# Tail scores of two heads from one shared low-part product, with the decay added by VectorE and head 1's operands stacked by GpSimd

## The chip, the cores and the metric

The kernel runs on one core of a Trainium2 chip. The metric is the device time of one execution in microseconds (us), the median of several runs. The engines are TensorE (PE in the profile), VectorE (DVE), ScalarE (ACT), GpSimd (POOL) and SyncE (SP, which here issues nearly all transfers).

## What is computed

Attention with a forget gate over 8 batches, 8 heads, 576 tokens and head size 64, and a mixing block with a feed-forward part on its output:

```
scores = (q @ k.T) / 8
cum    = cumsum(log(clip(f, 1e-4, 1)))                 # per head and token
scores = where(causal, -1e9, scores + cum[row] - cum[column])
attn   = softmax(scores); x = attn @ v                 # heads side by side: x is (8, 576, 512)
h      = (x.T @ U @ V).T;  u = x + h
out    = u + relu(u @ w_ch1) @ w_ch2
```

Results have the precision of float32. Where the kernel multiplies in the faster type fp32r, it splits an operand into a high part and the rest (the low part), and adds up the products.

## The kernel before, in words

Two heads of a batch make a pair; there are 32 pairs, p = 0 to 31. One call of `step(t)` is made of ten slots (`s`) and works on three pairs at once: scores of pair t, transposition and first values of the pair before, the rest of the one before that. In every slot PE also gets one unit of the feed-forward part of an earlier batch, where there is one (`filler`), or of a batch's mixing (`mixing`). The order of PE and SP is the order of the code; that of DVE, ACT and POOL comes from a scheduler at build time (SP's as well in steps 1 to 6).

The scores of a head are taken in four blocks of 128 query rows against the keys up to the diagonal (`score`, L379 on). The last 64 tokens of both heads, the **tail**, share one block of 128 rows, head 0 above head 1, against all 576 keys, in two halves of 288 columns (`score_tail`, L405 on; tile `St`).

Pairs 0 to 5 (p < NF = 6) multiply in full precision, from padded tiles `qk` that hold 64 rows of data, one row of ones and one of decay (L364). A tail half takes two products, one a head, which show as two records each. Pairs 6 to 31 multiply in fp32r, from two tiles `G[j]`, one a head, with four planes: plane 0 is the query's high part, plane 2 the key's high part in one half of the partitions and its low part in the other, plane 1 the query's low part and plane 3 the key's high part, with four rows of ones and decay in the free half (`parts`, L332 on, `place_decay`, L348 on). L367 multiplies planes 0 and 2, L368 planes 1 and 3. A tail half takes four such products, two a head. `parts` fills the planes by casts (L330, on ACT, or all on POOL in six steps) and subtractions on POOL (L345, L346). The decay rows come from the internal tensor `cumd` by SP (L351).

DVE then adds the mask, takes the row minimum of the negated scores and writes the sum back (L388, tail L414), ACT exponentiates (L396, tail L424) and frees the bank. In the first seven steps DVE also decodes the feed-forward weights (L72 to L89) from 64-bit words.

Of the kernel before, what the change touches and what calls it, by code (L numbers as in the profile page):

```python
# [21 lines left out]
P = 128  # L22
# [15 lines left out]
NX = 3  # L38
NF = 6


@with_exitstack
def tile_decay_attention_moe(ctx, tc, qk, v, f, U, V, w1, w2, out):
# [83 lines left out]
    COLS = tuple(slice(o, o + S) for o in AOFF)  # L127
    mask = att.tile([P, ZR + HW], F32, name="mask")
    nc.vector.memset(mask, 0.0)
    blank = mask[:, 0:256].bitcast(mybir.dt.bfloat16)  # L130
# [11 lines left out]
    def clear_operands():  # L142

        for j in range(2):
            g = G[j].bitcast(F32)
            tc.keep_in_program_order(nc.gpsimd.memset(g[OTH[j], 1, COLS[j]], 0.0))
            tc.keep_in_program_order(nc.gpsimd.memset(g[OTH[j], 3, COLS[j]], 0.0))
            tc.keep_in_program_order(nc.gpsimd.memset(g[ORW[j] : ORW[j] + 4, 1, COLS[j]], 1.0))
            tc.keep_in_program_order(nc.gpsimd.memset(g[ORW[j] : ORW[j] + 4, 3, COLS[j]], 1.0))
            z0 = (AOFF[j] + S) % 640  # L150
            tc.keep_in_program_order(nc.gpsimd.memset(g[:, 0:2, z0 : z0 + 64], 0.0))


    def decay_log():
        fr = sb.tile([B * H, S], F32, tag="xT", name="fr")
        fl = sb.tile([B * H, S], F32, tag="cr", name="fl")
        return fr, fl, G[0][0 : B * H, :, 0:S], sb.tile([B * H, 2, S], F32, tag="VS", name="dq")
# [54 lines left out]
    def load_w(u):  # L212
# [4 lines left out]
        if kind == "w2":  # L217

            spare = xn[NX - 1].rearrange("p c d -> p (c d)").bitcast(I32)
            if fc % 2:  # L220
                raw, a = spare[:, 1536:2560], sb.tile([P, 512], I32, tag="w2a", name=f"stg{u}")
# [94 lines left out]
    def load_v(p):  # L316
        vr = sb.tile([P, NM + 1, P], F32, tag="vr", name=f"vr{p}")
        st[p]["vr"] = vr.rearrange("p c (j d) -> p c j d", j=2)
        nc.sync.dma_start(vr[:, 0:NM], v[p, 0:MAIN].rearrange("(c p) d -> p c d", p=P))
        for r in range(2):  # L320
            nc.sync.dma_start(vr[64 * r : 64 * r + 64, NM], v[p, MAIN:S])

# [9 lines left out]
    def parts(p, j, engines):  # L332
# [12 lines left out]
        pin(el.tensor_tensor(g[oth, 2, cols], k[oth], gf[oth, 2, cols], op=ALU.subtract))  # L345
        pin(em.tensor_tensor(g[own, 1, cols], q[own], gf[own, 0, cols], op=ALU.subtract))  # L346

    def place_decay(p, j, cm=None):  # L348
        o, r = ORW[j], j * B * NHP + p
        if cm is None:  # L350
            nc.sync.dma_start(G[j].bitcast(F32)[o : o + 4, 1:4:2, COLS[j]], cumd[r])  # L351
            return
# [52 lines left out]
    def score_tail(p, x):  # L405
        z = st[p]
        ps = bank_s(p, f"St{p}_{x}")
        cols = slice(hw * x, hw * x + hw)
        for j in range(2):
            qk_mm(ps[:, :hw], p, ATAIL[j], cols, j == 0, j == 1, j)  # L410
        z["tl"].append(ps)

        def top():
            nc.vector.tensor_tensor_reduce(  # L414
                ps[:, :hw], ps[:, :hw], mask[:, x * ZR : x * ZR + hw], scale=-SCALE,
                scalar=3.0e38 if x == 0 else z["nm"][:, 8:9],
# [149 lines left out]
    def values(p, j):  # L566
# [247 lines left out]
    with tc.manual_schedule(engines=None):  # L814
# [43 lines left out]
    def step(t):  # L858
# [11 lines left out]
        for s in range(6 + 2 if last else SLOTS):  # L870
# [839 lines left out]
```

## Time and profile before

| what | value |
|---|---|
| median of 3 runs | 1192.13 us (1192.12 to 1192.14) |
| the profiled execution's own time | 1192.27 us |
| its span in the profile | 1190.5 us |
| instructions in it | 23774 |
| share of the chain that ended last | PE 85%, DVE 8%, ACT 4%, issue 2%, POOL 1% |

The span runs from the first to the last instruction that the profile shows; the own time has some 1.8 us around it. The chain is followed back from the last instruction, at each step to what released it.

### The profile page before, as it was taken

How to read it: one execution, taken by the hardware profiler on the slowest of the kernel's cores; microseconds unless marked ns; L12 is line 12 of the kernel's file. 1: busy time of each engine (PE TensorE's matmuls, PEld its weight loads, DVE VectorE, ACT ScalarE, POOL GpSimd, SP SyncE). 2: the span in 40 equal slices, each digit the busy share in tenths (PEclk: the TensorE clock that was granted, in tenths of full speed). 3: DMA queues.
4: the chain of work that ended last, by engine and by line, in shares of the span. 5: the costliest groups of instructions: out<-in, count | busy, mean ns of one | idle time of the engine just before them, and what ended most of it. 6: DMA issues, size and time to landing. Idle time of an engine off the chain costs nothing.

```text
span 1190.5 us, 23774 instructions
## 1 busy us (share of the span) xinstructions
PE 1173.5 (99%) x8400; PEld 1080.8 (91%) x8400; DVE 906.1 (76%) x2188; ACT 752.7 (63%) x2046; POOL 561.1 (47%) x588
## 2 busy tenths in 40 slices
PE   8999999999999999999999999999999999999998
PEld 5888899999899989989989997788999999999998
DVE  8988777677777677777676699966777767777675
ACT  8887786766868758767765577344454544545443
POOL 3315565546637447555553000024565555555554
PEclk9999999999999999999999999999999999999999
DMA  5754234434426425426332344542424344243421
GB/s 161 196 147 153 78 98 146 116 82 142 121 74 174 114 58 163 111 74 179 82 84 96 108 142 155 155 112 95 131 89 124 97 135 138 94 107 102 130 54 36
DMA packets 81431, 138.47 MB, mean 116 GB/s; under 512 B 8768, under 2 KB 46144, under 8 KB 79264
## 3 DMA queue, kind: packets, MB, share of 16 engines
q1 hardware_dynamic: 79680, 128.16, 36.1%
q0 software_dynamic: 1152, 8.39, 3.8%
q8 instruction: 66, 1.08, 0.4%
q14 instruction: 53, 0.43, 0.1%
q10 hardware_dynamic: 480, 0.40, 0.1%
HBM read 101.08 MB, written 35.78 MB: 115 GB/s over the span
## 4 chain that ended last, share of the span: by engine, by line
PE 85%; DVE 8%; ACT 4%; issue 2%; POOL 1%; DMA 0%; SPq 0%; ACTq 0%; DVEq 0%; POOLq 0%
PE N L1321 12%; PE B L775 12%; PE A L756 11%; PE A L1301 9%; PE B L1301 7%; PE V L579 6%; PE T L467 4%; PE S L367 3%; PE S L368 3%; PE O L1402 2%; PE B L1321 2%; PE V L544 2%; PE Tt L645 2%; PE S L364 1%; PE T_v L485 1%
## 5 line engine op out<-in xcount | busy, mean ns | idle before, releaser
L396 ACT ACTIVATE P<-S,nm 128x128 f32<-128x128 f32 (+3 forms) x256 | 138.0, 541 | 53.7 <-DVE nm L388 52.7
L199 POOL TENSOR_TENSOR hb<-xn,hb 128x256 fp32r<-128x256 f32 x136 | 111.6, 840 | 126.3 <-ACT hb L196 113.4
L388 DVE CUSTOM_DVE_ANT_0 S<-S,mask 128x128 f32<-128x128 f32 (+3 forms) x256 | 125.7, 497 | 52.5 <-PE S L368 48.6
L330 POOL CAST G<-qk 64x576 fp32r<-64x576 f32 (+1 forms) x76 | 50.6, 679 | 172.4 <-PE St L368 63.8
L756 PE MATMUL A<-uh,w1h 128*128 128x256 f32 (+1 forms) x384 | 119.8, 312 | 0.0
L756 PE MATMUL A<-ul,w1h 128*128 128x256 f32 (+1 forms) x384 | 113.6, 296 | 0.0
L756 PE MATMUL A<-uh,w1l 128*128 128x256 f32 (+1 forms) x384 | 113.5, 296 | 0.0
L196 ACT CAST hb<-xn 128x256 fp32r<-128x256 f32 x136 | 51.7, 404 | 84.7 <-DVE xn L1307 45.5
L775 PE MATMUL B<-w2h,hh 128*128 128x512 f32 x216 | 88.2, 408 | 0.0
L446 DVE TENSOR_TENSOR PTl<-T,PTh 128x512 fp32r<-128x512 f32 (+1 forms) x156 | 78.4, 527 | 9.6 <-ACT PTh L443 8.6
L467 PE MATMUL T<-ident,P 128*128 128x128 f32 x544 | 85.3, 272 | 0.0
L775 PE MATMUL B<-w2l,hh 128*128 128x512 f32 x216 | 85.0, 394 | 0.0
L775 PE MATMUL B<-w2h,hl 128*128 128x512 f32 x216 | 84.6, 392 | 0.0
L1321 PE MATMUL N<-sw,hb 128*128 128x256 f32 x546 | 79.9, 282 | 0.0
L1321 PE MATMUL N<-b2h,hb 128*128 128x256 f32 x420 | 79.8, 282 | 0.0
L345 POOL TENSOR_TENSOR G<-qk,G 64x576 fp32r<-64x576 f32 x52 | 74.7, 1437 | 10.8 <-issue 4.1
L346 POOL TENSOR_TENSOR G<-qk,G 64x576 fp32r<-64x576 f32 x52 | 75.0, 1442 | 6.6 <-ACT G L330 5.0
L367 PE MATMUL S<-G 128*128 128x128 f32 x208 | 70.9, 345 | 4.5 <-ACT P L396 3.3
L756 PEld LDWEIGHTS A<-uh,w1h 128*128 128x128 f32 x384 | 72.9, 190 | 0.9 <-DVE hl L761 0.2
L756 PEld LDWEIGHTS A<-uh,w1l 128*128 128x128 f32 x384 | 73.1, 190 | 0.5
L756 PEld LDWEIGHTS A<-ul,w1h 128*128 128x128 f32 x384 | 72.9, 190 | 0.0
L1321 PEld LDWEIGHTS N<-sw,hb 128*128 128x128 f32 x546 | 71.6, 190 | 0.0
(342 smaller groups left out, 3995.1 us busy)
## 6 DMA issues: line engine op xcount, KB each, us to landing
qk<-in_qk_dram SPq DMA_DIRECT2D x104, 288.0 KB
direct<-ud SPq DMA_DIRECT2D x48, 256.0 KB
sr<-in_w_dram SPq DMA_DIRECT2D x20, 512.0 KB
vr<-in_v_dram SPq DMA_DIRECT2D x32, 256.0 KB
accd<-ost SPq DMA_DIRECT2D x32, 256.0 KB
xn<-accd SPq DMA_DIRECT2D x8, 1024.0 KB
out_dram<-xn SPq DMA_DIRECT2D x30, 256.0 KB
ud<-uh SPq DMA_DIRECT2D x7, 1024.0 KB
```

The costliest lines, as they stand in the source:

```text
L199: leng.tensor_tensor(dl, src, dh.bitcast(F32), op=ALU.subtract)
L345: pin(el.tensor_tensor(g[oth, 2, cols], k[oth], gf[oth, 2, cols], op=ALU.subtract))
L346: pin(em.tensor_tensor(g[own, 1, cols], q[own], gf[own, 0, cols], op=ALU.subtract))
L367: nc.tensor.matmul(ps, G[j][:, 0, c0 : c0 + P], G[j][:, 2, cols], start=first, stop=False)
L388: newest["top"] = nc.vector.tensor_tensor_reduce(ps[:, :w], ps[:, :w], mask[:, 512 - w : 512], scale=-SCALE, scalar=3.0e38, op0=ALU.add, o ...
L396: nc.scalar.activation(pt, ps[:, :w], AF.Exp, bias=z["nm"][:, col : col + 1], scale=-1.0, accum_out=z["sm"][:, col : col + 1])
L446: defer(2, lambda: nc.vector.tensor_tensor(dstl, src, dsth.bitcast(F32), op=ALU.subtract))
L467: nc.tensor.transpose(tp[:, P * x : P * x + P], z["P"][j][i][:, P * c : P * c + P], ident)
L756: nc.tensor.matmul(ps[:, :nt], wt[:, fc, c], ut[:, c, sl], start=m == 0, stop=m == 3 * NDC - 1)
L775: nc.tensor.matmul(ps, ht[:, fc, P * x : P * x + P], wt[:, fc], start=fc == 0 and m == 0, stop=fc == NA - 1 and m == 2,)
L1301: nc.tensor.matmul(ps, a[x][:, c], b[y][:, c], start=start and m == 0, stop=m == 5, skip_group_check=not start)
L1321: nc.tensor.matmul(ps[:, y], a[p_][:, P * y : P * y + P], w[q_], start=start and y == 0 and m == 0, stop=stop and y == 1 and m == 2,)
```

## The change

- The tail of pairs 2 to 5 takes one full-precision product a half, from `both_q` (both heads' tail queries on a block diagonal) and `both_k` (head 0's keys above head 1's). POOL copies them there (`join_tail`).
- The tail of pairs 6 to 31 takes three fp32r products a half: the two of planes 0 and 2 as before, and one that multiplies the low parts of both heads' queries by both heads' keys. For that the low part of head 1's tail queries is written into plane 1 of `G[0]` (so one subtraction is split in two), and a transfer stacks head 0's keys into plane 3 of `G[1]` (`join_keys`).
- The decay of the tail is no longer a part of the product. From pair 2 on a base row of each head (the cumulated decay against that of token 511, times -8) is spread over 64 partitions of the mask by two transfers a pair (`load_tail`), POOL adds the triangle (`lean_mask`), and DVE's mask addition brings it in.
- The stacked keys lie where head 1's decay rows stood. These come into spare rows of `G[0]` by an own transfer and are copied by POOL behind the tail, in two pieces (`next_decay`).
- At the start POOL clears a part of the mask, copies the triangle, clears `both_q` and works out the base rows, which SP stores. Five of ten clearing writes of `G` go, some tiles get other places, and the value loads of pairs 1 to 5 keep their place in the program.

```diff
     mask = att.tile([P, ZR + S], F32, name="mask")
-    nc.vector.memset(mask, 0.0)
+    nc.vector.memset(mask[:, 0:640], 0.0)
+    lean = mask[:, ZR:]
...
+        if j == 0:
+            pin(em.tensor_tensor(g[own, 1, cols], q[own], gf[own, 0, cols], op=ALU.subtract))
+            return
+        pin(em.tensor_tensor(G[0][own, 1, S : S + TAIL], q[own, 0:TAIL], gf[own, 0, TAIL:P], op=ALU.subtract))
+        pin(em.tensor_tensor(g[own, 1, P:], q[own, TAIL:S], gf[own, 0, P:], op=ALU.subtract))
+
+    def load_tail(p):
+        if not NO <= p < NP:
+            return
+        for j in range(2):
+            r = j * B * NHP + p
+            nc.sync.dma_start(lean[64 * j : 64 * j + 64], based[r : r + 1].broadcast_to([64, S]))
+
+    def join_tail(p):
+        if not NO <= p < NF:
+            return
+        for j in range(2):
+            q, k = st[p]["qk"][j]
+            at = AOFF[1] if j else MAIN
+            nc.gpsimd.tensor_copy(both_q[OWN[j], 64 * j : 64 * j + TAIL], q[0:64, at : at + TAIL])
+            nc.gpsimd.tensor_copy(both_k[OWN[j]], k[0:64])
+
+    def lean_mask(p):
+        if NO <= p < NP:
+            nc.gpsimd.tensor_tensor(lean[:, MAIN:S], lean[:, MAIN:S], tri, op=ALU.add)
+
+    ASIDE = slice(96, 100)
+
+    def next_decay(lo, hi):
+        nc.gpsimd.tensor_copy(G[1][0:4, 3, AOFF[1] + lo : AOFF[1] + hi], G[0].bitcast(F32)[ASIDE, 3, lo:hi])
+
+    def join_keys():
+        nc.sync.dma_start(G[1].bitcast(F32)[OTH[1], 3, COLS[1]], G[0].bitcast(F32)[OWN[0], 3, COLS[0]])
...
-            nc.sync.dma_start(G[j].bitcast(F32)[o : o + 4, 1:4:2, COLS[j]], cumd[r])
+            g = G[j].bitcast(F32)
+            if j == 0:
+                nc.sync.dma_start(g[o : o + 4, 1:4:2, 0:MAIN], cumd[r][:, :, 0:MAIN])
+                nc.sync.dma_start(g[ASIDE, 3, 0:MAIN], cumd[B * NHP + p][:, 1, 0:MAIN])
+            else:
+                nc.sync.dma_start(g[o : o + 4, 1, P:], cumd[r][:, 0, TAIL:S])
...
-        for j in range(2):
-            qk_mm(ps[:, :hw], p, ATAIL[j], cols, j == 0, j == 1, j)
+        if p < NO:
+            for j in range(2):
+                qk_mm(ps[:, :hw], p, ATAIL[j], cols, j == 0, j == 1, j)
+        elif p < NF:
+            nc.tensor.matmul(ps[:, :hw], both_q, both_k[:, cols], start=True, stop=True)
+        else:
+            at = [slice(AOFF[j] + cols.start, AOFF[j] + cols.stop) for j in range(2)]
+            for j in range(2):
+                nc.tensor.matmul(ps[:, :hw], G[j][:, 0, ATAIL[j] : ATAIL[j] + P], G[j][:, 2, at[j]], start=j == 0, stop=False)
+            nc.tensor.matmul(ps[:, :hw], G[0][:, 1, MAIN : MAIN + P], G[1][:, 3, at[1]], start=False, stop=True)
...
+        nc.gpsimd.tensor_copy(tri, lean[:, MAIN:S])
+        nc.gpsimd.memset(both_q, 0.0)
+        nc.gpsimd.tensor_scalar(fl, fr, fr[:, MAIN - 1 : MAIN], -8.0, op0=ALU.subtract, op1=ALU.mult)
+        nc.sync.dma_start(based, fl)
...
                 place_decay(p, 1)
+                join_keys()
+            if s == 2 and ps_:
+                at(5, lambda: lean_mask(p))
...
+            if s == 5 and ps_ and p >= NF:
+                at(5, lambda: next_decay(0, HW))
+            if s == 6 and ps_ and p >= NF:
+                at(5, lambda: next_decay(HW, MAIN))
...
+            if s == 9 and ps_:
+                at(5, lambda: join_tail(p + 1))
...
+            if s == 8 and ps_:
+                load_tail(p + 1)
```

How the change moves instructions shows in three places. The first is PE at the tail of pair 8 (`St_0` and `St_1` are its halves, `Ty` and `T_v` transpositions of the pair before). Before:

```order
L367 MATMUL St_0_1863<-G_91 128x288
L368 MATMUL St_0_1863<-G_91 128x288
L367 MATMUL St_0_1863<-G_92 128x288
L368 MATMUL St_0_1863<-G_92 128x288
L507 MATMUL Ty_6_1868<-ident,Ptl_1631 64x128
L509 MATMUL Ty_6_1868<-ident,xT_1680 64x128
L367 MATMUL St_1_1880<-G_91 128x288
L368 MATMUL St_1_1880<-G_91 128x288
L367 MATMUL St_1_1880<-G_92 128x288
L368 MATMUL St_1_1880<-G_92 128x288
L485 MATMUL T_v<-ident,Ptl_1631 128x128 x4
```

The same place on PE now:

```order
L462 MATMUL St_0_1904<-G_91 128x288
L462 MATMUL St_0_1904<-G_92 128x288
L463 MATMUL St_0_1904<-G_92,G_91 128x288
L560 MATMUL Ty_6_1908<-ident,Ptl_1665 64x128
L562 MATMUL Ty_6_1908<-ident,xT_1716 64x128
L462 MATMUL St_1_1921<-G_91 128x288
L462 MATMUL St_1_1921<-G_92 128x288
L463 MATMUL St_1_1921<-G_92,G_91 128x288
L538 MATMUL T_v<-ident,Ptl_1665 128x128 x4
```

Each half has three products for four, and nothing else on PE moves there.

The second is POOL in the same step, from the tail of pair 8 to the preparation of head 1 of pair 9 (`xh`, `xl` belong to the mixed rows, `sm` to the softmax sums). Before:

```order
L330 CAST G_91<-qk_0_2015 64x576
L630 TENSOR_TENSOR xh_2152<-xn_105,xh_2152 64x128
L631 TENSOR_TENSOR xl_2153<-xn_105,xh_2152 128x512
L436 TENSOR_TENSOR sm_2005<-sm_2005 128x1
L346 TENSOR_TENSOR G_91<-qk_0_2015,G_91 64x576
L345 TENSOR_TENSOR G_91<-qk_0_2015,G_91 64x576
L330 CAST G_92<-qk_1_2194 64x576
L346 TENSOR_TENSOR G_92<-qk_1_2194,G_92 64x576
L345 TENSOR_TENSOR G_92<-qk_1_2194,G_92 64x576
```

The same place on POOL now:

```order
L383 CAST G_92<-G_91 4x288
L383 CAST G_92<-G_91 4x224
L683 TENSOR_TENSOR xh_2199<-xn_108,xh_2199 64x128
L684 TENSOR_TENSOR xl_2200<-xn_108,xh_2199 128x512
L489 TENSOR_TENSOR sm_2049<-sm_2049 128x1
L353 TENSOR_TENSOR G_91<-qk_0_2061,G_91 64x576
L351 TENSOR_TENSOR G_91<-qk_0_2061,G_91 64x576
L378 TENSOR_TENSOR mask<-mask,tri 128x64
L336 CAST G_92<-qk_1_2241 64x576
L355 TENSOR_TENSOR G_91<-qk_1_2241,G_92 64x64
L356 TENSOR_TENSOR G_92<-qk_1_2241,G_92 64x512
L351 TENSOR_TENSOR G_92<-qk_1_2241,G_92 64x576
```

The cast of `G_91` has moved ahead of the tail and two small copies stand in its place; the mask addition comes ahead of head 1's cast, and head 1's query residual is in two pieces.

The third is POOL in the early pairs, from the last weight decoding on POOL to the mixed rows of the first pair. Before:

```order
L76 TENSOR_TENSOR stg_160<-stg_160 128x512
L78 TENSOR_TENSOR w1l<-stg_160,w1h 128x512
L458 MEMSET PT_474 64x128
L630 TENSOR_TENSOR xh_543<-xn_104,xh_543 64x128
L631 TENSOR_TENSOR xl_544<-xn_104,xh_543 128x512
```

The same place on POOL now:

```order
L78 TENSOR_TENSOR stg_164<-stg_164 128x512
L80 TENSOR_TENSOR w1l<-stg_164,w1h 128x512
L373 COPY both_q<-qk_98 64x64
L374 COPY both_k<-qk_98 64x576
L373 COPY both_q<-qk_99 64x64
L374 COPY both_k<-qk_99 64x576
L511 MEMSET PT_488 64x128
L378 TENSOR_TENSOR mask<-mask,tri 128x64
L683 TENSOR_TENSOR xh_557<-xn_107,xh_557 64x128
L684 TENSOR_TENSOR xl_558<-xn_107,xh_557 128x512
```

Four copies and a mask addition stand there for each of the pairs 2 to 5.

## Rows read from the trace of the kernel before

**Rows 1.** Engine table: busy us, share of the span, instructions.

```profile
PE 1173.5 (99%) x8400; PEld 1080.8 (91%) x8400; DVE 906.1 (76%) x2188; ACT 752.7 (63%) x2046; POOL 561.1 (47%) x588
```

**Rows 2.** Stretches: length, busy us of PE, PEld, DVE, ACT, POOL; granted clock, DMA.

```profile
15.00:35.00 20.00, 18.46 (x115) 14.30 (x114) 19.70 (x63) 15.90 (x51) 2.98 (x3) 1.00 0.68 203
35.00:85.00 50.00, 49.85 (x344) 41.10 (x342) 45.92 (x138) 41.22 (x125) 13.96 (x22) 1.00 0.63 169
...
300.00:640.00 340.00, 338.54 (x2382) 311.01 (x2382) 252.52 (x730) 248.66 (x712) 189.34 (x190) 1.00 0.40 113
```

**Rows 3.** PE's waits, whole span: us in total, times, longest.

```profile
PE S L367 <- ACT P L396: 3.3, 5, 1.1
```

**Rows 4.** Timeline of PE, a late pair's tail: start, us, instruction.

```profile
312.15 0.29 PE L367 MATMUL St<-G 128*128 128x288 f32 x1
312.28 0.30 PE L368 MATMUL St<-G 128*128 128x288 f32 x1
...
312.68 0.27 PE L507 MATMUL Ty<-ident,Ptl 128*64 128x128 f32 x1
```

**Rows 5.** Chain that ended last, around 300 us: start, us, what.

```profile
296.06 0.97 ACT Ptl L424 x4
...
300.46 0.44 PE S L367
```

**Rows 6.** The same chain at pair 2's tail.

```profile
38.83 0.97 PE St L364 x4
```

**Rows 7.** Groups on POOL, 92 to 642 us: busy, mean ns, idle before, releaser.

```profile
L346 POOL TENSOR_TENSOR G<-qk,G 64x576 fp32r<-64x576 f32 x52 | 75.0, 1442 | 6.6 <-ACT G L330 5.0 <-DMA qk<-in_qk_dram 0.3
...
L330 POOL CAST G<-qk 64x576 fp32r<-64x576 f32 x51 | 34.7, 680 | 112.8 <-PE St L368 63.8 <-PE S L368 36.8 <-PE S L367 9.7
L631 POOL TENSOR_TENSOR xl<-xn,xh 128x512 fp32r<-128x512 f32 x26 | 33.6, 1292 | 2.0
...
L630 POOL TENSOR_TENSOR xh<-xn,xh 64x128 fp32r<-64x128 f32 x26 | 11.8, 453 | 30.7 <-ACT xh L629 30.0
L436 POOL TENSOR_TENSOR sm<-sm 128x1 f32<-128x1 f32 x26 | 5.0, 191 | 3.9 <-ACT Ptl L424 3.7
```

**Rows 8.** Tile G, clearing writes on POOL: shortest, median, longest ns.

```profile
L147 POOL MEMSET G<- x2: 569/571/573, 54.8 to 57.7; 64x576 f32 x2
...
L149 POOL MEMSET G<- x2: 567/570/572, 56.1 to 58.7; 4x576 f32 x2
```

**Rows 9.** Timelines of DVE and POOL in the early pairs.

```profile
17.80 0.42 DVE L72 TENSOR_SCALAR stg<-stg 128x512 int32<-128x512 int32 x1
...
23.13 1.31 POOL L78 TENSOR_TENSOR w1l<-stg,w1h 128x512 fp32r<-128x512 f32 x1 [2.21 <-ACT w1h L77]
23.22 1.50 DVE L72 TENSOR_SCALAR stg<-stg 128x512 int32<-128x512 int32 x1
...
69.48 0.72 DVE L88 TENSOR_SCALAR xn<-xn 128x512 int32<-128x512 int32 x1 [0.55 <-ACT stg L83]
```

**Rows 10.** Timelines of POOL and PE, a mixing step and a plain one.

```profile
290.50 1.44 POOL L345 TENSOR_TENSOR G<-qk,G 64x576 fp32r<-64x576 f32 x1
292.71 0.29 PE L368 MATMUL St<-G 128*128 128x288 f32 x1
...
303.97 0.66 POOL L330 CAST G<-qk 64x576 fp32r<-64x576 f32 x1 [3.37 <-PE S L367]
```

**Rows 11.** Timeline of PE, pair 6, from its tail to head 1's first scores.

```profile
101.28 0.27 PE L507 MATMUL Ty_None<-ident,Ptl 128*64 128x128 f32 x1
...
104.84 0.33 PE L367 MATMUL S<-G 128*128 128x128 f32 x1
```

**Rows 12.** Transfers: issue on SP (timeline), one in the chain, the page's load.

```profile
297.10 1.24 SPq L294 DMA_DIRECT2D qk<-in_qk_dram  x2
...
124.36 3.20 DMA qk<-in_qk_dram
...
xn<-ud POOLq DMA_DIRECT2D x7, 1024.0 KB, 8.3
```

More of the change, by code (lines that the diff above doesn't have):

```diff
@@ L39 @@
 NF = 6
+NO = 2
 @with_exitstack
@@ L48, in tile_decay_attention_moe @@
     accd = nc.dram_tensor("accd", (NG, NM, P, DM), F32, kind="Internal").ap()
+    based = nc.dram_tensor("based", (B * H, S), F32, kind="Internal").ap()
     def words(ap):
@@ L127, in tile_decay_attention_moe @@
     COLS = tuple(slice(o, o + S) for o in AOFF)
-    mask = att.tile([P, ZR + HW], F32, name="mask")
-    nc.vector.memset(mask, 0.0)
+    mask = att.tile([P, ZR + S], F32, name="mask")
+    nc.vector.memset(mask[:, 0:640], 0.0)
+    lean = mask[:, ZR:]
+    tri = att.tile([P, TAIL], F32, name="tri")
+    both_q = att.tile([P, P], F32, name="both_q")
+    both_k = sb.tile([P, S], F32, tag="xT", name="both_k")
     blank = mask[:, 0:256].bitcast(mybir.dt.bfloat16)
@@ L146, in clear_operands @@
             tc.keep_in_program_order(nc.gpsimd.memset(g[OTH[j], 1, COLS[j]], 0.0))
-            tc.keep_in_program_order(nc.gpsimd.memset(g[OTH[j], 3, COLS[j]], 0.0))
-            tc.keep_in_program_order(nc.gpsimd.memset(g[ORW[j] : ORW[j] + 4, 1, COLS[j]], 1.0))
-            tc.keep_in_program_order(nc.gpsimd.memset(g[ORW[j] : ORW[j] + 4, 3, COLS[j]], 1.0))
+            if j == 0:
+                tc.keep_in_program_order(nc.gpsimd.memset(g[OTH[j], 3, COLS[j]], 0.0))
             z0 = (AOFF[j] + S) % 640
@@ L154, in decay_log @@
     def decay_log():
-        fr = sb.tile([B * H, S], F32, tag="xT", name="fr")
-        fl = sb.tile([B * H, S], F32, tag="cr", name="fl")
+        fr = sb.tile([P, 640], F32, tag="xh", name="fr")[0 : B * H, 0:S]
+        fl = sb.tile([P, S], F32, tag="cr", name="fl")[0 : B * H]
         return fr, fl, G[0][0 : B * H, :, 0:S], sb.tile([B * H, 2, S], F32, tag="VS", name="dq")
@@ L220, in load_w @@
             if fc % 2:
-                raw, a = spare[:, 1536:2560], sb.tile([P, 512], I32, tag="w2a", name=f"stg{u}")
+                raw, a = spare[:, 1536:2560], sb.tile([P, S], I32, tag="cr", name=f"stg{u}")[:, 0:512]
             else:
@@ L318, in load_v @@
         st[p]["vr"] = vr.rearrange("p c (j d) -> p c j d", j=2)
-        nc.sync.dma_start(vr[:, 0:NM], v[p, 0:MAIN].rearrange("(c p) d -> p c d", p=P))
+        pin = tc.keep_in_program_order if 0 < p < NF else lambda x: x
+        pin(nc.sync.dma_start(vr[:, 0:NM], v[p, 0:MAIN].rearrange("(c p) d -> p c d", p=P)))
         for r in range(2):
-            nc.sync.dma_start(vr[64 * r : 64 * r + 64, NM], v[p, MAIN:S])
+            pin(nc.sync.dma_start(vr[64 * r : 64 * r + 64, NM], v[p, MAIN:S]))
     def make_vs(p):
@@ L345, in parts @@
         pin(el.tensor_tensor(g[oth, 2, cols], k[oth], gf[oth, 2, cols], op=ALU.subtract))
-        pin(em.tensor_tensor(g[own, 1, cols], q[own], gf[own, 0, cols], op=ALU.subtract))
+        if j == 0:
[25 more added lines that the diff above has]
+        nc.sync.dma_start(G[1].bitcast(F32)[OTH[1], 3, COLS[1]], G[0].bitcast(F32)[OWN[0], 3, COLS[0]])
     def place_decay(p, j, cm=None):
@@ L350, in place_decay @@
         if cm is None:
-            nc.sync.dma_start(G[j].bitcast(F32)[o : o + 4, 1:4:2, COLS[j]], cumd[r])
+            g = G[j].bitcast(F32)
+            if j == 0:
+                nc.sync.dma_start(g[o : o + 4, 1:4:2, 0:MAIN], cumd[r][:, :, 0:MAIN])
+                nc.sync.dma_start(g[ASIDE, 3, 0:MAIN], cumd[B * NHP + p][:, 1, 0:MAIN])
+            else:
+                nc.sync.dma_start(g[o : o + 4, 1, P:], cumd[r][:, 0, TAIL:S])
             return
@@ L414, in top @@
             nc.vector.tensor_tensor_reduce(
-                ps[:, :hw], ps[:, :hw], mask[:, x * ZR : x * ZR + hw], scale=-SCALE,
+                ps[:, :hw], ps[:, :hw], lean[:, hw * x : hw * x + hw], scale=-SCALE,
                 scalar=3.0e38 if x == 0 else z["nm"][:, 8:9],
@@ L573, in values @@
             z["xT"] = sb.tile([P, S], F32, tag="xT", name=f"xT{p}")
-        z["cr"] = sb.tile([D, S], F32, tag="cr", name=f"cr{p}_{j}")
+        z["cr"] = sb.tile([P, S], F32, tag="cr", name=f"cr{p}_{j}")[0:D]
         VS, xT, cr = z["VS"], z["xT"], z["cr"]
@@ L822, in tile_decay_attention_moe @@
         pad(1, 0)
+        nc.gpsimd.memset(mask[:, 640:], 0.0)
         nc.gpsimd.affine_select(mask[:, DG : DG + P], mask[:, DG : DG + P], [[-1, P]], ALU.is_ge, MASKED, base=0, channel_multiplier=1)
@@ L825, in tile_decay_attention_moe @@
             nc.gpsimd.affine_select(
-                mask[64 * j : 64 * j + 64, ZR + HW - TAIL :], mask[64 * j : 64 * j + 64, ZR + HW - TAIL :],
+                lean[64 * j : 64 * j + 64, MAIN:S], lean[64 * j : 64 * j + 64, MAIN:S],
                 [[-1, TAIL]], ALU.is_ge, MASKED, base=0, channel_multiplier=1,
```

## The prediction

> **What bounds the kernel now.** I read the engine table first: TensorE (PE) is busy 1173.5 us of the span, VectorE (DVE) 906.1, ScalarE (ACT) 752.7, GpSimd (POOL) 561.1 [rows 1]. The table of stretches says where this holds [rows 2]. [...] In the early pairs, 35 to 85 us, PE is full too (49.85 of 50), but DVE is close behind with 45.92; from 15 to 35 us DVE leads (19.70 of 20, PE 18.46). A PE saving in the early pairs is therefore only worth what DVE lets through. The list of PE's waits is short: the heaviest, for the score bank that ACT empties, is 3.3 us in five waits over the whole run [rows 3].
>
> **The late pairs (6 to 31): three products for four.** The PE timeline of one tail (the last 64 tokens' scores of both heads) shows its four products starting at 312.15, 312.28 and so on, and the next work at 312.68 [rows 4]: 0.53 us for four, 0.133 us each, whatever the 0.29 us beside one says, since products overlap. The change drops one of four in each of two column halves of 26 pairs: 52 x 0.133 = 6.9 us. What it does not give: in the steps where a batch's mixing starts, the chain leaves PE and runs over DVE and ACT, and PE then waits for it (the chain from 296.06 through ACT to PE at 300.46) [rows 5]. A tail ahead of such a wait saves nothing, the wait grows by as much. I count the five waits [rows 3] as five lost pairs: 5 x 0.27 = 1.3 us, leaving 5.6 (ends: 4.7 with eight pairs lost, one for each batch, 6.9 with none).
>
> **The early pairs (2 to 5): one product for two.** In the chain four matmul records, which are two full-precision products, take 0.97 us [rows 6]. Each half of a tail keeps one of its two products: 8 x 0.485 = 3.9 us of PE. For that POOL stacks queries and keys: per pair two copies of 64x576 at 0.68 [rows 7], two of 64x64 and one 128x64 addition to the mask. For the small ones the nearest rows are 0.19 (128x1) and 0.45 (64x128); I take 0.3. That is 2.3 us a pair, 9.0 for four, less five clearing writes of 0.57 that are gone [rows 8], so about 6.2 us more POOL work inside the DVE-heavy stretch. DVE pays for some of it: a DVE operation that takes 0.42 alone took 1.50 when it met a POOL subtraction of 1.31, and another took 0.72 [rows 9]. So DVE loses between 0 and 0.8 us for each us of POOL; these two collisions and the ones that left no mark make me take 0.35: 2.2 us. Then PE needs 45.95 us in this stretch and DVE 48.1, the 50 us shrink to about 48.3, and 1.7 us are gained (ends: 3.9 if nothing collides, 0.9 us lost at 0.8).
> [...]
>
> **The tail's new hand-offs.** Four things now have to be in time; I cost them at 0.3 us together.
> First, POOL's preparation of head 1 ahead of the tail. Its order is now mask addition, cast, the split residual (64x64 and 64x512, 0.3 + 1.29 for 1.44), key residual: about 0.45 us more. In a plain step the cast starts at 303.97 and the three operations end near 307.5, 4.6 us ahead of the tail at 312.15 [rows 4, 10]. In six steps, those in which POOL makes all casts, the last operation begins at 290.50 and ends at 291.94, and the product that reads it sits at 292.71 in the new order [rows 10]: 0.77 us of cover against 0.45 more work. If it falls short it costs some tenths in six steps, up to 1 us.
> Second, the decay rows of head 1, which POOL copies behind the tail into the place of the stacked keys. Partitions cost nothing (4x576 and 64x576 are both written in 0.57 us) [rows 8], so at 0.68 per 576 columns the 288 and 224 columns take 0.34 and 0.26. The first copy only waits for the tail's first half; between that and head 1's first score product lie 3.5 us even in the tightest step I found (101.28 to 104.84) [rows 11]. POOL waited for the tail at this point before as well, for a cast that now leaves the place early: hidden. Behind the copies POOL has the residuals of the mixed rows, which idle 30.7 us for ACT anyway [rows 7]. If POOL were still busy with a 1.29 us subtraction, the copy would be in time all the same.
> Third, the transfer that stacks head 0's keys under head 1's. It leaves when the last score product of the pair before is done, about when the cast starts (303.97), and is needed at 312.4: 8.4 us. SP issues each transfer in 0.6 us, and a 288 KB load took 3.2 us in the chain [rows 12]; this one moves 144 KB, so 2 x 0.6 + 3.2 = 4.4 us. Hidden with 4 us to spare.
> Fourth, the base row that is spread into the mask by two transfers a pair, issued at slot 8, and POOL's addition behind them. They are wanted some 3 us later by POOL, which is waiting for PE then; a delay of 1 to 2 us goes into the 4.6 us of cover above. SP gets four more issues per pair, 2.4 us of a step of some 17.5; behind them stand the loads for the next pair, which are several us early.
> DVE's tail minimum reads a row of the same width as before, no change. The start is reordered (a mask part cleared by POOL, one more 64x576 POOL operation, one more store): 0, with ends of 0.7 us to either side, half of such an operation (1.44) [rows 7].
>
> **Sum.** The profiled execution took 1192.27 us, 0.14 over the median of 1192.13. From the median: 1192.1 - 5.6 - 1.7 + 0.3 = **1185.1 us**. Of a difference under 0.2% (2.4 us) a measurement of this kernel could not tell much, so the borders are 1189.7 and 1194.5.
>
> **Rivals.**
> *All of it shows* (0.17). DVE keeps up in the early pairs because its work is not in PE's way, and the mixing waits don't grow: 1192.1 - 6.9 - 3.9 = 1181.3. For it: PE was never idle from 35 to 85 us. Against: DVE has 4 us of room there and 3.9 are asked of it, with POOL's collisions on top.
> *The early pairs give nothing* (0.13). POOL's copies block DVE at 0.8 for each us, the early stretch gets 0.9 us longer, the start costs its 0.7: 1192.1 - 5.6 + 0.9 + 0.3 + 0.7 = 1188.4. It decides from a loss of about 0.6 for each us of POOL, where DVE's need reaches PE's old 49.85. [...]
> *The gain is waited away* (0.06). Head 1's first products find POOL's decay copy late by about as much as was saved, 0.2 to 0.3 us a pair: 1190 to 1192. That needs POOL to be over 3.5 us behind at the tail, in most steps; its idle time of 112.8 us ahead of the cast [rows 7] speaks against it.
> *The stacked keys come late, slower* (0.06). If the key transfer, queued behind others, took as long as the 1 MB load that the page shows (8.3 us to landing) [rows 12], it would land 1.2 + 8.3 = 9.5 us after the cast's start, 1.1 us behind the tail's third product at 8.4; in 26 pairs 28.6 us, less the gains of 5.6 and 1.7: 1213. It decides from 8.7 us on, where the wait of 0.27 eats the saving of a pair. Against it: the DMA engines are 40% busy [rows 2], and the transfer is a seventh of that load.
> That the change does not remove the products can be excluded: the order on PE shows it.
>
> **How the numbers follow.** My forecast has 0.58. Faster by over 0.2%: 0.58 + 0.17 and 0.10 of the early-pairs rival = 0.85. Within 0.2%: the rest of that rival and the waited-away one, 0.09. Slower: 0.06. The range goes from the full gain with a slightly better start, 1181.0, to the early pairs giving nothing with six short waits, 1189.6; it leaves out the last two rivals and some of their neighbours.
>
> **What would show it.** In the profile after: 156 fp32r tail records for 208 and 32 fp32 ones for 48; tails of a late pair of 0.4 us per half, their starts still 0.133 apart; PE full from 300 to 640 with no new wait at the tail or at head 1's first product; DVE over 95% busy from 35 to 85 us, and the transposition behind the first fp32r tail half (101.28 now) some 1 to 2 us earlier. If it is 4 us earlier, the DVE term was wrong; if it isn't earlier at all, POOL's collisions cost more. PE waits on POOL or on a DMA ahead of the tail in every step would make the hand-offs wrong.

## The result, and the profile after

The changed kernel takes 1199.59 us (median of six runs, 1198.44 to 1202.06) against 1192.09 for the kernel before (1192.02 to 1192.14): a ratio of 1.0068, 95% interval 1.0055 to 1.0081. It is slower; the forecast was 1185.1, faster. The profiled execution took 1199.65, its span 1197.8 us. The runs also lie 3.6 us apart, where before they agreed within 0.12.

The engine table of the kernel after, against [rows 1]:

```profile
PE 1172.3 (98%) x8332; PEld 1074.0 (90%) x8332; DVE 914.3 (76%) x2188; ACT 752.8 (63%) x2046; POOL 604.4 (50%) x711
```

POOL has 43 us more to do, while PE is barely below its 1173.5 us. The stretches (columns as in [rows 2]) and two short pieces of them:

```profile
35.00:85.00 50.00, 46.59 (x316) 38.23 (x315) 45.50 (x130) 38.02 (x118) 16.81 (x30) 0.97 0.69 181
100.00:145.00 45.00, 39.37 (x287) 35.25 (x288) 36.85 (x94) 33.67 (x95) 27.18 (x32) 0.96 0.43 125
300.00:640.00 340.00, 335.48 (x2337) 305.06 (x2336) 254.87 (x728) 248.65 (x709) 212.28 (x257) 1.00 0.50 135
60.00:64.00 4.00, 4.00 (x21) 3.91 (x21) 2.90 (x4) 0.25 (x1) 2.97 (x7) 0.57 0.38 110
135.00:139.00 4.00, 3.71 (x22) 3.71 (x23) 2.19 (x7) 1.89 (x7) 0.00 (x0) 0.57 0.02 4
```

From 100 to 145 us the kernel before read:

```profile
100.00:145.00 45.00, 40.99 (x312) 37.41 (x311) 37.70 (x100) 34.33 (x98) 22.54 (x21) 1.00 0.34 103
```

PE is idle for longer than before in all three stretches, and in the two short pieces its granted clock is 0.57 in the mean of 4 us (0.50 from 60.5 to 63.5 and from 135.5 to 138.5 us). The products themselves went as planned: on the PE timeline of a late tail, the half that began at 312.15 and ended at 312.68 before [rows 4] now takes 0.40 us.

```profile
320.35 0.42 PE L462 MATMUL St<-G 128*128 128x288 f32 x2
320.62 0.29 PE L463 MATMUL St<-G,G 128*128 128x288 f32 x1
320.75 0.27 PE L560 MATMUL Ty<-ident,Ptl 128*64 128x128 f32 x1
```

Where the time went is seen by following one event through the run. The table gives, in us, when the first product of a pair's tail (the first `St` record on PE) starts in a profiled execution, less its start before (37.59 for pair 2, 312.15 for pair 16, 630.43 for pair 31). The kernels named e1 to e15 are the experiments below. A row is one execution: those of e1, e13 and e14 are the fastest of their kernels (1192.08, 1185.94 and 1184.80 us against medians of 1193.52, 1186.39 and 1186.94).

| pair | 2 | 4 | 6 | 7 | 8 | 12 | 16 | 20 | 28 | 31 |
|---|---|---|---|---|---|---|---|---|---|---|
| after | -0.26 | +3.61 | +2.26 | +2.63 | +5.39 | +5.52 | +8.20 | +8.23 | +8.11 | +7.73 |
| e1 late half | -0.74 | -0.56 | -0.64 | -0.36 | +0.89 | +0.89 | +1.48 | +1.15 | +0.59 | +0.31 |
| e2 early half | -0.26 | +5.80 | +4.45 | +4.73 | +4.74 | +4.99 | +5.40 | +4.91 | +5.28 | +5.26 |
| e8 | -0.71 | -0.13 | -0.30 | -1.29 | -1.22 | -1.68 | -1.98 | -2.70 | -3.13 | -4.02 |
| e11 | -0.26 | +0.16 | -1.17 | -0.88 | +0.37 | +1.89 | +3.39 | +2.89 | +4.14 | +3.67 |
| e13 | -0.73 | -0.56 | -0.63 | -1.75 | -1.70 | -2.17 | -2.66 | -3.35 | -5.15 | -6.02 |
| e14 | -0.26 | -0.48 | -1.67 | -2.39 | -3.19 | -3.43 | -3.93 | -4.46 | -6.20 | -7.14 |

In plain steps a pair mostly gains 0.17 to 0.28 us on before, in every kernel with three products (pairs 8 to 10 after: +5.39, +5.12, +4.86). So the saving is real, and most of it and more is lost in three places: 3.0 us just ahead of pair 4's tail, 2.8 between pairs 7 and 8, 3.2 between pairs 15 and 16. PE's timeline of the kernel after shows a wait in each:

```profile
58.66 3.06 PE L597 MATMUL V<-vr,PTh 128*128 128x64 f32 x20 [1.49 <-DMA vr<-in_v_dram]
...
135.29 0.35 PE L698 MATMUL Tt<-xh,Us 128*64 128x128 f32 x1 [1.20 <-DVE PTl L499]
...
298.97 0.40 PE L462 MATMUL St<-G 128*128 128x288 f32 x1 [1.09 <-POOL G L351]
```

The first waits for a transfer (V of pair 2), the second for DVE, the third for POOL. Behind the first and the second lie the two falls of the clock: by an estimate from these rows, 4 us at 0.57 cost 4 x 0.43 = 1.7 us each. The third place has no fall; much of the rest of its 3.2 us is in short waits, the longest 0.62 us for DVE (`xT`, 316.30) and 0.42 for the decay rows (310.59). The wait for `xT` is new and comes back; over the run it reads

```profile
PE T_v L520 <- DVE xT L652: 2.4, 6, 0.6
```

### The profile page after: what moved, and what is told of

Its sections match the earlier page's. It is cut to its first block, busy times and chain, and to the rows that moved or that the text cites. A ratio compares the mean times of both kernels' runs of the same rounds, so it can differ in the third digit from the quotient of the medians.

```text
span 1197.8 us, 24066 instructions
## 1 busy us (share of the span) xinstructions
PE 1172.3 (98%) x8332; PEld 1074.0 (90%) x8332; DVE 914.3 (76%) x2188; ACT 752.8 (63%) x2046; POOL 604.4 (50%) x711
## 4 chain that ended last, share of the span: by engine, by line
PE 62%; DVE 8%; ACT 2%; issue 1%; SPq 0%; DMA 0%; POOL 0%; DVEq 0%; ACTq 0%
PE N L1390 12%; PE A L1370 9%; PE B L828 8%; PE A L809 7%; PE B L1370 7%; PE V L632 3%; PE O L1471 2%; PE B L1390 2%; PE T L520 2%; PE S L412 2%; PE S L413 1%; PE O L1234 1%; DVE S L433 1%; PE Tt L698 1%; PE Tx L663 1%
## 5 line engine op out<-in xcount | busy, mean ns | idle before, releaser
L351 POOL TENSOR_TENSOR G<-qk,G 64x576 fp32r<-64x576 f32 x52 | 74.4, 1431 | 10.5 <-issue 4.1
L496 ACT CAST PTh<-T 128x512 fp32r<-128x512 f32 (+1 forms) x156 | 68.2, 469 | 4.0 <-PE T L520 3.3
```

What stands on the lines that cost most here:

```text
L496: defer(0, lambda: nc.scalar.copy(dsth, src))
```

## Experiments

The first question was which half loses.

```diff
 # e1_late_only, on the changed kernel
-NO = 2
+NO = 6
```

> The change without its early half: pairs 2 to 5 make their tails as before, with two fp32 products a half, no stacked copies, and the base rows come from pair 6 on; pairs 6 to 31 as changed. Theory (each late and each early part pays for itself where it stands; what was lost between the tails of pairs 2 and 4, 3.9 us, is the early half's): this gives that back and loses the early half's saving of 0.5 to 0.8 us a pair, so about 1197 us, still slower than before, with the stretches of pairs 7 to 8 (+2.8 us) and 15 to 16 (+3.2 us) as in the changed kernel. Rival (the early half is the whole loss, because everything later follows from a start that was pushed back): under 1190 us. Rival (the early half gains as forecast): above 1200 us.

```diff
 # e2_early_only, on the changed kernel
-        if p < NO:
+        if p < NO or p >= NF:
...
-                join_keys()
...
-            if s == 5 and ps_ and p >= NF:
-                at(5, lambda: next_decay(0, HW))
-            if s == 6 and ps_ and p >= NF:
-                at(5, lambda: next_decay(HW, MAIN))
...
```

> The change's early half alone: pairs 2 to 5 with one stacked product a half, their base rows and POOL copies; from pair 6 on the four products, the ones beside the decay rows and the causal mask as before, with the mask set back once by POOL at pair 6. Theory: the lost stretch between the tails of pairs 2 and 4 shows again, with the late V load and 3.4 us of clock at 0.50, so 1193 to 1196 us and nothing at pairs 7 to 8 and 15 to 16. Rival (the early half gains, as forecast 1.7 us): 1190 to 1191 us. Rival (the late half is what delays the V load): same as before within 1 us.

```diff
 # e3_no_base_rows, on the changed kernel
-        if not NO <= p < NP:
+        if not NO <= p < 0:
             return
...
-        if NO <= p < NP:
+        if NO <= p < 0:
             nc.gpsimd.tensor_tensor(lean[:, MAIN:S], lean[:, MAIN:S], tri, op=ALU.add)
```

> The whole change, but the base rows are neither loaded (two transfers of 147 KB in the SBUF for each of pairs 2 to 31) nor added to the triangle by POOL (0.32 us each), so the tails' scores lack the decay between a query and its base: the products and the rest of POOL's work are as changed. Theory (transfers that land late start the waits): all three lost stretches go but for the mixing step's 1.1 us, and 1186 to 1191 us is left. Rival (POOL's copies and casts that collide with VectorE are what costs): 30 x 0.32 us of POOL fewer give back 1 to 3 us, so 1196 to 1199 us.

The late half alone takes 1193.52 us (ratio 1.0016, 1.0006 to 1.0025), the early half 1197.04 (1.0040, 1.0025 to 1.0055). Their losses of 1.6 and 5.1 us make 6.7 of the 7.5: both halves lose, mostly each for itself. For e1 both rivals fall, but 1197 was 3.5 us too high: it loses 1.25 us between pairs 7 and 8 and 0.70 between 15 and 16, where 2.8 and 3.2 were expected, and in the profiled execution its clock stays at 1.00. e2 shows the lost stretch ahead of pair 4 and next to nothing at the other two (0.01 and 0.21), as expected, but loses 1 us more than its 1193 to 1196; its rivals fall. Without base rows the kernel takes 1197.33 (1.0047, 1.0027 to 1.0068; five runs, 1195.19 to 1201.77). The 2.3 us that it is below the change are not clear of the noise; the time lies well short of the 1186 to 1191 expected if transfers were the whole cause and inside the rival's range, and this profile shows another cause. DVE and POOL in a mixing step of e3:

```profile
288.80 1.28 POOL L742 TENSOR_TENSOR ul<-full,uh 128x512 fp32r<-128x512 f32 x1
...
288.81 1.30 DVE L490 TENSOR_SCALAR sm<-sm 128x9 f32<-128x9 f32 x1 [0.92 <-ACT P L441]
```

DVE adds 1e-9 to nine numbers a partition and needs 1.30 us for it, ending with POOL's subtraction. In this profile it does so beside that subtraction five times (from 199.58 to 627.63), and the tail that comes next, of pairs 11, 15, 23, 27 and 31, loses 0.9 to 1.1 us each time. Over the run the same 32 instructions read (shortest, median, longest ns), before, after, and, as the reciprocal that reads the same numbers, in e6 below:

```profile
L437 DVE TENSOR_SCALAR sm<-sm x32: 170/282/1396, 20.1 to 644.2; 128x9 f32<-128x9 f32 x32
```
```profile
L490 DVE TENSOR_SCALAR sm<-sm x32: 165/424/1271, 19.6 to 651.7; 128x9 f32<-128x9 f32 x32
```
```profile
L437 DVE RECIPROCAL rv<-sm x32: 200/215/218, 20.1 to 642.2; 128x9 f32<-128x9 f32 x32
```

The addition is stretched up to eightfold, the reciprocal never, though 18 of its 32 in e6 lie wholly beside a POOL instruction. So the addition was taken away, from three kernels, beside a fourth that moves the early half's start:

```diff
 # e4_no_eps (changed kernel), e5_late_no_eps (e1), e6_before_no_eps (before)
-        nc.vector.tensor_scalar(sm[:, 0:9], sm[:, 0:9], 1e-9, None, op0=ALU.add)
 # e7_from_pair_4 (changed kernel)
-NO = 2
+NO = 4
```

> The whole change without VectorE's addition of 1e-9 to the sums of exponentials (each sum holds the exponential of its own row's largest score, so it is at least 1, and in float32 the addition changes nothing). That instruction has 9 numbers a partition and takes 0.17 us where POOL is idle, but 1.25 us where a POOL subtraction of 128x512 runs (15.6 us over 32 of them, against 10.1 us before the change). Theory (POOL's added work makes VectorE's SBUF-only instructions wait, and TensorE behind them): 2 to 4 us come back, 1195.5 to 1197.5 us. Rival (those waits of VectorE are covered, transfers alone cost): 1199 to 1200 us, no change.

> The late half alone (as e1_late_only) without the same addition. Theory: the late half loses only at the steps where VectorE stands in that addition until POOL is done (1.27 us at 113.7, 0.98 at 306.7, 1.21 at 325.0 in the profile of e1_late_only), so 1 to 3 us come back from 1193.5, to 1190.5 to 1192.5 us, and the times of the runs lie closer together. Rival (it is the transfers of base rows and keys): stays at 1193 to 1194 us.

> The kernel before, without the same addition. Its 32 take 10.1 us, 4.6 us over 0.17 each, with one long one (1.40 us at 114.8). Theory (the long waits come with POOL's added work): 0 to 1 us less than before, 1191.0 to 1192.0 us. Rival (this addition costs whatever POOL does): 3 us less or more, as large a gain as in e4_no_eps.

> The change with the stacked product from pair 4 on, in place of pair 2: no base rows are loaded for pairs 2 and 3, so the transfers at 32.5 and 41.7 us are gone, and those that remain are issued behind the V load of 52.9 us. Theory (the base rows ahead of the V load and of the decay stores delay it, and the clock falls behind that wait): the 3.0 us lost before the tail of pair 4 do not show, pairs 4 and 5 still save 0.6 to 0.8 us each, so at most 1 us from e1_late_only either way, 1192.5 to 1194.5 us. Rival (POOL's copies of queries and keys are the cost, whichever pair they are for): half of the early half's loss stays, 1195.5 to 1197 us.

The addition was worth 2.6 us in the whole change (1196.97 us; 1.0041, 1.0031 to 1.0052), 3.3 in its late half (1190.24, just below its range; 0.9986, 0.9977 to 0.9996) and 1.8 in the kernel before (1190.17; 0.9986, 0.9976 to 0.9995). PE's waits for `xT`, 2.4 us in the kernel after and 1.9 in e1, are gone in the profiles of e4 and e5: that is one way in which the addition reached PE. The runs of the late half lie hardly closer together, 4.0 us apart for 5.1. The last gain is more than expected: before, too, it was caught once for 1.40 us at 114.80, under POOL's subtraction of 114.40 to 116.16. Without it the late half stands where the kernel before stands without it: this instruction explains 1.5 us, not the missing 5.6.

e7 missed. It takes 1197.14 us though no base row is issued ahead of the V load. Its profile has the same wait and then a clock of 0.50, and SP's longest wait between 36 and 56 us shows a cause that is not the base rows:

```profile
57.69 2.70 PE L597 MATMUL V<-vr,PTh 128*128 128x64 f32 x20 [1.35 <-DMA vr<-in_v_dram]
```
```profile
SPq L402 <- DMA xn<-in_w_dram: 2.5, 1, 2.5
```

SP stood 2.5 us behind a 512 KB load of weights, and V left at 54.43 where it left at 52.45 before; in e1 that wait was 1.0 us, V left at 52.96, and PE did not wait. Of SP's 618 transfers in the trace of the kernel after, 602 use the semaphore of the one issued eight places ahead (eight semaphores in turn), and 563 first wait for the semaphore that they use. So V arrives with little slack, and an added or reordered transfer can move it. The runs of e7 fall into 1193.7 to 1193.9, 1195.8 and 1197.1 to 1197.7; whether V's arrival is what parts them is not shown.

In the kernel after V is late in another way. Its load left SP at 52.86, hardly later than before and earlier than in e1; it was under way for longer. SP's timeline and the stretch from 54 to 58 us, before and then after:

```profile
52.45 0.53 SPq L319 DMA_DIRECT2D vr<-in_v_dram  x1
54.00:58.00 4.00, 4.00 (x32) 3.64 (x31) 3.74 (x11) 3.71 (x13) 3.88 (x8) 1.00 0.50 146
```
```profile
52.86 0.53 SPq L325 DMA_DIRECT2D vr<-in_v_dram  x1
54.00:58.00 4.00, 2.77 (x19) 2.09 (x17) 3.79 (x15) 4.00 (x14) 1.88 (x4) 1.00 1.03 251
```

The DMA engines were busy 1.03 of that stretch, where they were 0.50 before. In the three profiles with the four base rows of pairs 2 and 3 and the late load of V (after, e2, e4) PE waited for V until 5.3 to 5.8 us after its load had left; in those without these rows in which PE waited (e3, e5, e7, e8) until 2.8 to 3.3 us. The 512 KB weight load ahead of V left at 49.91 instead of 47.32; that V then stood behind it in the DMA engines fits this, but is not shown by itself.

Four more kernels, three against one place each and one (e10) that joins two of them and frees the order of the early V loads:

```diff
 # e8_decode_on_pool, on e5: last subtraction of the last W2 block
...
-            sub.tensor_tensor(l[rows], af[rows], h.bitcast(F32)[rows], op=ALU.subtract)
+            (low or sub).tensor_tensor(l[rows], af[rows], h.bitcast(F32)[rows], op=ALU.subtract)
...
 # e9_rows_before_keys, on e5: slot of place_decay(p + 1, 0)
+            if s == 6 and NF < nxt_p < NP:
+                place_decay(p + 1, 0)
             if s == 6 and ps_ and p:
                 load_qk(p + 1, 1)
-            if s == 7 and NF <= nxt_p < NP:
+            if s == 7 and nxt_p == NF:
 # e10_three_mends: e8 + e9, and in load_v
-        pin = tc.keep_in_program_order if 0 < p < NF else lambda x: x
+        pin = lambda x: x
 # e11_v_early, on the changed kernel
+        if p == 2:
+            vr = xn[1].rearrange("p c d -> p (c d)")[:, 0 : (NM + 1) * P].rearrange("p (c d) -> p c d", d=P)
...
-            if s == 1 and pa and 0 < a <= NF:
+            if (s == 5 and p == 2) or (s == 1 and pa and 0 < a <= NF and a != 2):
```

> e5_late_no_eps with one instruction moved: the last subtraction of the last block of W2 (128x512, two operands in SBUF) goes from VectorE to POOL, which is idle for 3.5 us just behind its own work there. In e5 it took 1.86 us on VectorE (129.13), for as long as POOL's subtraction at 129.02 ran, where it takes 0.67 in the kernel without the change; behind it PTl came late and TensorE waited 1.20 us at 131.84. Theory (an instruction of VectorE with both operands in SBUF stands still while POOL computes): the 1.2 us lost between the tails of pairs 7 and 8 go, 1188.5 to 1189.5 us. Rival (VectorE has too much to do there, so that another comes late instead): 1190 to 1191 us.

> e5_late_no_eps with the decay rows of the next pair's first head issued by SP one step earlier, ahead of the next pair's second head of queries and keys, which is all that moves. Theory (in a mixing step SP stands behind the store of ul, which waits for POOL, and the transfers of the decay rows, two for a pair where there was one, land last and hold TensorE 0.5 us at 217.0 and 0.47 us at 552.8): about 0.5 us come back at each of pairs 12, 16 and 28, so 1188.5 to 1190 us. Rival (the later queries and keys of the second head hold POOL in its place): 1190 to 1192 us.

> The edits of e8 and e9 together, and the V loads of the early pairs no longer held in program order, as in the kernel before. Theory: the two gains add (1.2 and about 1 us), and the wait for V at 57 us (0.8 us in e5, none before) goes: 1186.5 to 1188.5 us, the fastest of all kernels here. Rival (the gains overlap, or a clock fall remains): 1189 to 1191 us.

> The whole change, with V of pair 2 loaded half a step earlier into a place of its own (rows of the second batch's X, which are free until pair 4). Theory (the base rows push the V load back behind the decay stores, TensorE waits for it 1.5 us at 58.7 and then has 3.4 us of granted clock at 0.50): that wait and that clock fall go, so 2 to 3.5 us less than the change, 1196 to 1197.5 us. Rival (TensorE then waits for VectorE and POOL at the same place, because POOL's copies are what is late): 1198.5 to 1200 us.

e8 takes 1187.83 us (0.9964, 0.9951 to 0.9977): 2.4 us under e5, and the place between pairs 7 and 8 is gone (+0.07 instead of +1.24). Only these 1.2 us were expected; in its profile V also came earlier (a wait of 0.17 us for 0.78 in e5), which no edit of e8 aimed at. The same subtraction in the kernel before, in the kernel after with POOL beside it, then e8 on POOL and PE:

```profile
127.86 0.68 DVE L78 TENSOR_TENSOR w2l<-stg,w2h 128x512 fp32r<-128x512 f32 x1
```
```profile
132.59 1.85 DVE L80 TENSOR_TENSOR w2l<-stg,w2h 128x512 fp32r<-128x512 f32 x1
...
132.48 1.42 POOL L351 TENSOR_TENSOR G<-qk,G 64x576 fp32r<-64x576 f32 x1
```
```profile
130.05 1.29 POOL L80 TENSOR_TENSOR w2l<-stg,w2h 128x512 fp32r<-128x512 f32 x1
...
130.18 0.28 PE L697 MATMUL Tt<-xh,Us 128*64 128x128 f32 x1
```

A DVE subtraction with both operands in SBUF, 0.68 us before, took 1.85 and ended 0.54 us behind the POOL instruction that it met; on POOL itself it costs 1.29 us that nobody waits for, and `Tt` has no wait left.

e11 takes 1195.45 us, 4.1 under the change, half a microsecond more than expected, and settles the first place: it is V's arrival. V's products start without a wait and the clock stays up:

```profile
56.86 2.34 PE L600 MATMUL V<-xn,PTh 128*128 128x64 f32 x20
```
```profile
58.00:64.00 6.00, 6.00 (x50) 5.21 (x49) 4.91 (x12) 3.73 (x13) 4.05 (x9) 1.00 0.61 162
```

e9 is a clear miss, 1208.93 us, and e10 with it (1205.53). PE's waits and SP's timeline of e9:

```profile
PE St L462 <- POOL G L351: 15.8, 6, 2.8
```
```profile
208.68 0.67 SPq L393 DMA_DIRECT2D G<-cumd  x1
212.91 0.27 SPq L394 DMA_DIRECT2D G<-cumd  x1
213.23 1.14 SPq L299 DMA_DIRECT2D qk<-in_qk_dram  x2
```

The rows for head 1 overwrite what POOL's second decay copy behind the tail still reads (that copy begins at 212.52), so their transfer stood until 212.91, and the keys that used to leave at 209.84 (e5) left behind it at 213.23. PE waited 15.8 us for POOL's preparation of head 1, in six mixing steps. But in this step that wait ends at 207.57, so these later keys are not its cause. More moved than the expectation says: the build-time scheduler put POOL in another order in all six, with both `ul` subtractions ahead of head 1's residuals, where e5 has one. POOL in e9:

```profile
199.73 1.29 POOL L741 TENSOR_TENSOR ul<-full,uh 128x512 fp32r<-128x512 f32 x1
200.99 1.57 POOL L204 TENSOR_TENSOR VS<-vr,VS 128x640 fp32r<-128x640 f32 x1
202.53 1.27 POOL L741 TENSOR_TENSOR ul<-full,uh 128x512 fp32r<-128x512 f32 x1
```

So e9 and e10 say nothing on what earlier rows are worth by themselves. Why the rows were late the next kernels took up:

```diff
 # e12_whole_mended: e11 with the edits of e4 and e8
 # e13_store_last, on e8; e14_whole_store_last: the same on e12
-            defer(7, use, 3)
+            defer(7, use, 9 if 0 < b < B - 1 else 3)
 # e15_before_mended: the kernel before with the edits of e4, e8 and e13
```

> The whole change with V of pair 2 loaded early (as e11_v_early), without the addition of 1e-9, and with the last subtraction of the last W2 block on POOL (as e8_decode_on_pool). Theory (the early half saves about 0.5 us net once V is there in time: -1.17 us at the tail of pair 6 in e11 against -0.64 in e1): 1187 to 1188 us, 0 to 1 us below e8. Rival (POOL's copies and the base rows cost more than two products save, in whatever order): 1188.5 to 1191 us.

> e8_decode_on_pool with the stores of uh and ul of a middle batch issued some slots later, behind the V load, the queries and keys and the decay rows of the next pair on SP, which until then stand behind the store of ul (SP stood still from 198.8 to 205.7 us in e5). Theory (late transfers of the decay rows cost the pairs after a mixing step): pairs 12, 16 and 28 lose 0.5 us less each, so 1186 to 1187.3 us. Rival (POOL's work there is what is late): 1187.5 to 1188.5 us, no change.

> e12_whole_mended with the stores of uh and ul issued later, as in e13_store_last: the whole change, early half too, with all mends. Theory (e12's loss at pairs 12, 16 and 28 is the store's; the early half itself is worth the 0.8 us by which e12 stood ahead of e8 at the tail of pair 8): 1185 to 1186.5 us, at or just below e13's 1186.4. Rival (the early half costs more than it saves): 1187 to 1189.5 us.

> The kernel before with the three mends of e13_store_last (no addition of 1e-9, the last subtraction of the last W2 block on POOL, the stores of uh and ul later), all products as before. Theory (the second and third mend only repair what the change spoiled, the first is worth 1.8 us there as in e6_before_no_eps): 1189.7 to 1190.5 us, so that the late half of the change is worth 3.5 to 4 us of its forecast 5.6 once the waits are gone. Rival (the mends help the kernel before as much): 1186 to 1187.5 us, the change worth nothing.

e13 takes 1186.39 us (0.9952, 0.9936 to 0.9969) and was right. SP's timeline in the step ahead of pair 12's tail, e5 and then e13:

```profile
198.32 0.46 SPq L782 DMA_DIRECT2D ud<-uh  x1
205.67 0.36 SPq L779 DMA_DIRECT2D ud<-ul  x1
206.12 0.46 SPq L782 DMA_DIRECT2D ud<-ul  x1
206.67 1.07 SPq L325 DMA_DIRECT2D vr<-in_v_dram  x1
...
211.21 0.67 SPq L393 DMA_DIRECT2D G<-cumd  x1
```
```profile
201.55 1.24 SPq L299 DMA_DIRECT2D qk<-in_qk_dram  x2
202.88 0.67 SPq L393 DMA_DIRECT2D G<-cumd  x1
```

SP no longer stands 7 us behind the store of `ul`, and the first decay rows leave 8.3 us earlier (5.6 of them against pair 12's tail, which itself comes 2.75 us earlier). Pair 28, which lost 0.80 us in e8 with a PE wait of 0.81 for `G<-cumd`, gains 0.25 in e13. The number was right by some luck: the expectation had 0.5 us at each of pairs 12, 16 and 28, and the profiles give 0.01, 0.18 and 1.05, with 0.29 at pair 24 and 0.46 that e13 was ahead at pair 7 already.

e12 takes 1190.68 us, in a range of 1188.21 to 1193.15, which spoke for its rival; with the store moved it is e14, 1186.94 us (0.9954, 0.9939 to 0.9969; four runs, 1184.80 to 1188.17), between its theory and its rival. PE's waits of e12 for the decay rows are

```profile
PE S L416 <- DMA G<-cumd: 2.6, 4, 0.9
```

and e14's profile has none. e14 and e13 are not told apart. e15 takes 1190.71 us (0.9987, 0.9978 to 0.9997), 0.2 above its range: of the mends only the missing addition helps the kernel before (e6 took 1190.17), and the rival falls.

## Why the prediction was wrong

The whole change, step by step: 1199.6 us; V early, 1195.5; DVE's two instructions that stood for POOL mended as well, 1190.7; the store moved as well, 1186.9. The kernel before with the mends that apply to it: 1190.7. So the change is worth about 4 us of the forecast 7.0 once these waits are mended, and they took more than that back: V's, those behind DVE's two instructions (of whose gain the kernel before has 1.5 us as well) and those behind the store.

**Late pairs: right in mechanism and size of a product.** 52 products went (156 records for 208), a half takes 0.40 us, a plain step gains 0.17 to 0.28. The term of 5.6 us measured 4.3 (e13 against e15): in e13 pairs after a mixing step still give less, pairs 12 and 16 lose 0.28 and 0.22 and pair 20 gains nothing, and pairs 6 and 8 gain nothing either. The subtraction of five pairs stood for such losses and was too small.

**Early pairs: mis-sized.** The forecast was 1.7 us. With V in time, e11 stands 0.53 us ahead of e1 at pair 6 (-1.17 against -0.64); its pairs 5 and 6 do gain 0.49 and 0.84, but pairs 2 and 3 lose 0.5 each against e1 ahead of that. That POOL's copies, which fall there, are the cause was not tried. At the end it is within the runs' spread (e14 against e13). DVE was at 45.50 of 50 us, not over 95%, and POOL's work from 35 to 85 us grew from 13.96 to 16.81 us, not by 6.2.

**The hand-offs are the step that failed**, costed at 0.3 us together. The first came much as forecast: POOL fell short by 1.09 us at 298.97, in one step of the six. The second (the copies) and the third (the stacked keys) never held PE; the slower rival did not happen. The fourth failed: "behind them stand the loads for the next pair, which are several us early". V of pair 2 has no such slack: before, its product started 4.3 us after its load had left (52.45 to 56.75), and such a load takes 2.8 us at the least where PE waited for it (e8). The kernel after puts four mask transfers and a store ahead of it, and its wait took with the clock about 4 us (e11). The decay rows of the next pair have none either in mixing steps, where SP stands behind the store of `ul`: 2.6 us of PE's waits in e12. The prediction looked for the delay at POOL's mask addition, where POOL does wait, up to 5.22 us (311.81) and mostly covered, and not at SP's other customers. None of these waits comes in every step, which was the sign that the prediction named; they come in single steps.

**DVE's waits for POOL were counted for the early pairs only, and as a mean.** The 0.35 us for each us of POOL was an estimate and is no property of the work. In the trace of the kernel after some 115 of 2188 DVE instructions take over 0.2 us more than their like do where POOL is idle, none of them with an operand in PSUM, where the scores stand; those that read scores there stay within 0.06 us of their own median, and the 32 reciprocals take 0.20 to 0.22 us. Two of these few stood ahead of what PE waits for, in the late pairs as well: the addition (up to 1.27 us for 0.17) and the subtraction of two operands in SBUF (1.85 us, 0.68 before). What sets them apart from the reciprocal, which has no operand in PSUM either, is not shown. Asking which instructions on PE's path have no operand in PSUM would have found them.

**The clock was in no step.** Both falls in the kernel after, to 0.50, follow a PE wait of over a microsecond (1.49 and 1.20 us).

What stays open: how much of the 4.1 us is the base rows', since V is late without them too (e3 has none and a wait of 0.68 us, e7 none ahead of V and 1.35). The pinned order of the loads is hardly it: in e10, without the pin, V's load leaves at 54.01, no earlier than in the pinned e1, e5, e8 and e13 (52.91 to 54.13), but that was only tried together with e9's edit. The later store was only tried on top of the other mends.

## What to carry to other kernels

Before moving work to GpSimd, list the VectorE instructions on TensorE's path that touch only SBUF, however small: one of nine numbers a partition took 1.30 us for 0.17 here, beside a GpSimd subtraction of 1.28 and ending with it. Before adding a transfer, read what stands behind it on the issuing queue and what that queue is itself waiting for. When a saving is real per piece but missing at the end, follow one event through all repetitions against the kernel before; the steps where the gap jumps are the places to mend.

## What the runs showed of the hardware

In these runs the granted clock fell to 0.50 after some short waits and not after others alike: after the 1.20 us wait at 135.29 it was 0.57 in the mean of 4 us (135 to 139 us), while after a wait of 1.39 us at 122.32 in the same execution it stayed at 1.00 (122 to 126 us), and e5 and e11 have the 1.20 us wait with the clock at 1.00 behind it (132 to 136 us). Why the runs of the changed kernel lie 3.6 us apart is not shown: the two slowest, 1202.06 and 1202.04 us, have mean clocks of 0.995 and 0.997, the fastest, 1198.44, has 0.996. The stretching of DVE did not go by size: 9 numbers a partition took 1.30 us beside POOL's 1.28, ending with it (e3), and the reciprocal of the same numbers never took over 0.22 (e6).
